# A transformer block in split fp32 on one core: weights loaded whole and split in place, in more places

## The chip, the cores and the metric

The kernel runs on one core of a Trainium2 chip. The metric is device time in microseconds (us) of one execution, as the median of several runs; lower is better. The core's engines take their instructions in program order, each its own: PE (TensorE: matmuls; "PEld" is its loading of the stationary operand), DVE (VectorE), ACT (ScalarE), POOL (GpSimd) and SP (SyncE, which here only issues transfers, DMAs). ACT and POOL issue DMAs too. Engines wait for each other through semaphores.

## The reference

```python
h = _layernorm(x) * (1 + ca) + sa
x = x + ga * (softmax_attention(h @ wqkv, 32 heads, scale 16 ** -0.5) @ wo)
h = _layernorm(x) * (1 + cb) + sb
x = x + gb * ((_silu(h @ w_gate) * (h @ w_up)) @ w_down)
```

`x` is 2048 × 512, there are 32 heads of 16, and the hidden width F of the feed-forward network (FFN) is 1792. The six rows `sa, ca, ga, sb, cb, gb` come from `silu(c) @ w_mod`. Everything is fp32.

## The kernel before

**Split products.** PE multiplies operands of a shorter float, called fp32r in the profile. To keep fp32's precision each operand is split into a high part (`hi`, the value rounded by a copy) and a low part (`lo`, the value minus `hi`). A product is then three matmuls: high by high, high by low, low by high. The helper `accumulate` lists them as the terms `(0,0), (0,1), (1,0)`, for the left and the right operand.

**Stages.** After layer norm and the q, k, v projections, attention works on 32 units: four chunks of 512 queries, times eight groups of four heads. A unit takes 16 key tiles. For each there are scores (L506, L479), a running maximum (DVE, L481), exponentials (ACT, L508) and the product with v (L521). A unit's end normalizes: a row of sums is inverted, stored, and loaded back spread over partitions (`rb`, DMA at L542). POOL then multiplies, `on` (L548), and stores (`o_dr`, L549). For the last unit ACT and DVE do that.

**FFN.** When a chunk's eight units are done, it gets the output projection with wo, a residual, a second layer norm, and the FFN. The FFN has 14 `gate_up` jobs, one for each 128 columns of F, and 7 pairs of `down` jobs, each pair with 256 rows of w_down; they go in the order gate_up 0, 1, 2, down 0, gate_up 3, 4, down 1, and so on to gate_up 13, down 6. A gate_up ends with a tanh on ACT (L773), products on DVE (L777, L779: `m`) and a split of `m` into `mid` (L781 high, L782 low): POOL does it for chunks 0 to 2, ACT and DVE for the last chunk and one more place. Down results are added to the residual at L793.

**Order.** The code's order is each engine's order; nothing else schedules. `plain(...)` emits attention alone, `filled(places, work)` emits four attention pairs and puts matmuls of the previous chunk's FFN between them. So the FFN of chunks 0 to 2 runs inside the attention of later units, and the last chunk's runs alone at the end, through `whole`, which calls `hook()` (the postponed splits of `m`) after each job. `at(i, f)` makes a function due at step i; `n` is the number of steps.

**Weights before.** During the attention of chunk 0 a generator, `split_weights`, runs on POOL: it loads the plain weights, multiplies wo and w_down by their rows `ga` and `gb`, splits all, and stores both halves to DRAM (`gu_dr`, `wd_dr`, `wo_dr`). Every chunk then loads both halves, 1 MB for each gate_up (both matrices), for each down pair and for each of two wo tiles. The loads stand on SP's queue: L652 for gate and up, one job ahead in two places (`bufs=2`); L657 for down, in one place, issued when the previous pair is done. In the last chunk gate and up have four places. The last chunk's input (`v_flat<-in_A_x`, L641) is loaded by POOL's queue, and used when the output projection is added.

Of the kernel before, what the change touches and what calls it, by code (L numbers as in the profile page):

```python
# [19 lines left out]
P = 128  # L20
S = 2048
D = 512
# [79 lines left out]
def block_kernel(ctx, tc, x, wqkv, wo, w_gate, w_up, w_down, c, w_mod, out):  # L102
# [32 lines left out]
    o_dr = dram.tile([NC, NG, P, CW], F32, name="o_dr")  # L135
    gu_dr = dram.tile([NF, P, 4, NK, P], F32, name="gu_dr")
    wd_dr = dram.tile([NF // FG, P, 2, FG, D], F32, name="wd_dr")
    wo_dr = dram.tile([NK // 2, P, 2, 2, D], F32, name="wo_dr")

# [434 lines left out]

    def split_weights():

        def raw(src, k):
            t = tile_mid().bitcast(F32)
            nc.gpsimd.dma_start(t.rearrange("p e c -> p (e c)").rearrange("p (k c) -> p k c", k=k), src)
            return t  # L580

        def parts(hi, lo, t):
            nc.gpsimd.tensor_copy(hi, t)
            nc.gpsimd.tensor_sub(lo, t, hi.bitcast(F32))

        def store(dst, w):
            nc.gpsimd.dma_start(dst, w.bitcast(F32))

        def cols(m):
            return slice(m * FG * P, (m + 1) * FG * P)  # L590

        srcs = [(wod[:, 2 * k:2 * k + 2, :], 2) for k in range(NK // 2)]
        for m in range(NF // FG):
            srcs += [(wgd[:, :, cols(m)], NK), (wud[:, :, cols(m)], NK), (wdd[:, m * FG:(m + 1) * FG, :], FG)]
        ahead = [raw(*srcs.pop(0)) for _ in range(2)]
        yield

        def following():
            if srcs:
                ahead.append(raw(*srcs.pop(0)))  # L600
            return ahead.pop(0)

        for k in range(NK // 2):
            t = following()
            nc.gpsimd.tensor_mul(t, t, ga_bc[:, None, :].to_broadcast([P, 2, D]))
            w = tile_gu()
            parts(as_wo(w)[:, 0], as_wo(w)[:, 1], t)
            store(wo_dr[k], as_wo(w))
            yield
        for m in range(NF // FG):  # L610
            ws = [tile_gu() for _ in range(FG)]
            for e in range(2):
                t = following()
                src = t.rearrange("p e c -> p (e c)").rearrange("p (k f c) -> p f k c", k=NK, f=FG)
                for f in range(FG):
                    parts(ws[f][:, 2 * e], ws[f][:, 2 * e + 1], src[:, f])
                    if e:
                        store(gu_dr[m * FG + f], ws[f])
                yield
            t = following()  # L620
            nc.gpsimd.tensor_mul(t, t, gb_bc[:, None, :].to_broadcast([P, FG, D]))
            w = tile_wd()
            parts(w[:, 0], w[:, 1], t)
            store(wd_dr[m], w)
            yield

    class Chunk:
        def __init__(self, ci, x2, oT, hT):
            self.ci, self.x2, self.oT, self.hT = ci, x2, oT, hT
            self.w, self.wd, self.mid, self.mv, self.nt = {}, {}, {}, None, []  # L630
            self.places, self.ahead, self.loaded = None, 1, set()
            self.jobs = [(gate_up, (0,)), (gate_up, (1,))]
            for m in range(NF // FG):
                if m:
                    self.jobs.append((gate_up, (2 * m + 1,)))
                if m + 1 < NF // FG:
                    self.jobs.append((gate_up, (2 * m + 2,)))
                self.jobs += [(down, (m, 0)), (down, (m, 2))]
# [4 lines left out]
        def load_wo(self, places=None):  # L643
            self.wo = places or [as_wo(tile_gu()) for _ in range(NK // 2)]
            for k, w in enumerate(self.wo):
                (nc.gpsimd if self.ci == last else nc.sync).dma_start(w.bitcast(F32), wo_dr[k])

        def load_gu(self, f):
            if f < NF and f not in self.loaded:
                self.loaded.add(f)  # L650
                self.w[f] = self.places[f % len(self.places)] if self.places else tile_gu()
                nc.sync.dma_start(self.w[f].bitcast(F32), gu_dr[f])  # L652

        def load_wd(self, m):
            if m < NF // FG:
                self.wd[m] = tile_wd()
                nc.sync.dma_start(self.wd[m].bitcast(F32), wd_dr[m])  # L657

# [130 lines left out]
    def down(ch, m, t0, outs, halves):  # L789
# [54 lines left out]
    def close_unit(u, i):  # L844
# [12 lines left out]
        if u % NG == NG - 1:  # L857
            if u // NG:
                at(i + 4, lambda: begin(u // NG))
                at(i + 5, lambda: chunks[u // NG].load_wo())  # L860
            at(i + 7, lambda: chunks[u // NG].load_o(nc.gpsimd))
            at(i + 9, lambda: chunks[u // NG].split_o())

    at(3, lambda: begin(0))
    at(UG - 2, lambda: chunks[0].load_wo())

    weights2 = split_weights()

    def after(i):
# [6 lines left out]
        if i == -2:  # L876
# [7 lines left out]
            load_q(2)  # L884
        if 0 <= i < UG and i % 16 in (3, 5, 8):
            next(weights2, None)
# [84 lines left out]
    at(n - 24, begin_last)  # L971
    at(n - 13, lambda: chunks[last].load_o(nc.gpsimd, range(NK - 1)))
    at(n - 11, lambda: chunks[last].split_o(range(NK - 1)))
    outs = [banks[b] for b in FBANKS]
    for ci in range(last):
# [11 lines left out]
        for _ in range(len(ch.jobs) - (KEEP if ci == last - 1 else 0)):  # L987
# [55 lines left out]
    run(whole(ch, ch.jobs))  # L1043
# [23 lines left out]
```

## Time and profile before

| what | us |
|---|---|
| median of 3 runs (1879.09 to 1879.83) | 1879.76 |
| profiled execution: span from its first to its last instruction | 1875.6 |
| median of the runs less that span (the profile gives no other time of the profiled execution) | 4.2 |
| PE busy in the span | 1846.7 |
| DVE busy | 1541.8 |
| ACT busy | 1252.4 |
| POOL busy | 415.3 |

The page gives for each engine its busy time, its share of the span and its number of instructions. A row of a group reads: line, engine, operation, output<-inputs, shapes, number, then busy us and mean ns of one, then the idle time just before them and what ended it. A row of the timeline reads: start, duration, engine, line, operation, number; in brackets the idle time before and what ended it. A row of the waits reads: engine, instruction, what it waited for, us in all, times, the longest. A transfer's row has the size and the us from issue to landing. In the program's time, attention without FFN work runs from about 210 to 540 us, the FFN of chunks 0 to 2 is mixed in until about 1750, and the last chunk's FFN takes 1752 to 1871.

### The profile page before, as it was taken

How to read it: one execution, taken by the hardware profiler on the slowest of the kernel's cores; microseconds unless marked ns; L12 is line 12 of the kernel's file. 1: busy time of each engine (PE TensorE's matmuls, PEld its weight loads, DVE VectorE, ACT ScalarE, POOL GpSimd, SP SyncE). 2: the span in 40 equal slices, each digit the busy share in tenths (PEclk: the TensorE clock that was granted, in tenths of full speed). 3: DMA queues.
4: the chain of work that ended last, by engine and by line, in shares of the span. 5: the costliest groups of instructions: out<-in, count | busy, mean ns of one | idle time of the engine just before them, and what ended most of it. 6: DMA issues, size and time to landing. Idle time of an engine off the chain costs nothing.

```text
span 1875.6 us, 41002 instructions
## 1 busy us (share of the span) xinstructions
PE 1846.7 (98%) x16996; PEld 1160.4 (62%) x16996; DVE 1541.8 (82%) x2558; ACT 1252.4 (67%) x2406; POOL 415.3 (22%) x498
## 2 busy tenths in 40 slices
PE   7999999999999999999999999999999999999999
PEld 5766444444455766666555667666554566667887
DVE  5548999999999888888999888889999988831643
ACT  4221888888887766777777776677878877674211
POOL 3000454456323211111133111111123011030200
PEclk9999999999999999999999999999999999999999
DMA  8855677766843534554454454453643446243642
GB/s 286 292 198 142 174 183 178 201 167 190 211 86 78 145 102 124 144 124 90 107 124 116 108 127 131 121 122 78 159 86 56 108 92 156 86 159 119 249 180 110
DMA packets 78854, 267.62 MB, mean 143 GB/s; under 512 B 17364, under 2 KB 22484, under 8 KB 57988
## 3 DMA queue, kind: packets, MB, share of 16 engines
q1 hardware_dynamic: 59820, 180.10, 33.0%
q0 software_dynamic: 18160, 84.10, 19.0%
q8 instruction: 133, 2.18, 0.5%
q10 hardware_dynamic: 688, 0.80, 0.1%
q14 instruction: 53, 0.43, 0.1%
HBM read 201.85 MB, written 62.13 MB: 141 GB/s over the span
## 4 chain that ended last, share of the span: by engine, by line
PE 95%; DVE 2%; ACT 2%; DMA 0%; issue 0%; SPq 0%; ACTq 0%; DVEq 0%
PE bank L521 26%; PE bank L506 22%; PE bank L719 19%; PE bank L479 10%; PE bank L729 7%; PE bank L209 7%; DVE mx L481 1%; PE bank L762 1%; PE bank L491 1%; PE bank L162 0%; PE bank L703 0%; DMA wm_ab<-in_w_mod 0%; DVE stt L745 0%; PE bank L279 0%; PE bank L493 0%; PE bank L492 0%
## 5 line engine op out<-in xcount | busy, mean ns | idle before, releaser
L481 DVE TENSOR_REDUCE mx<-bank 128x1 f32<-128x512 f32 x2048 | 1286.5, 682 | 119.5 <-PE bank L479 72.4
L479 PE MATMUL bank<-kop,qop 48*128 48x512 f32 x2048 | 748.0, 432 | 3.6 <-DVE mx L481 3.4
L506 PE MATMUL bank<-qop,kop 50*128 50x512 f32 x2048 | 742.1, 427 | 4.6 <-ACT pt__20499 L508 0.5
L506 PEld LDWEIGHTS bank<-qop,kop 50*128 50x128 f32 x2048 | 347.0, 184 | 305.6 <-issue 63.3
L479 PEld LDWEIGHTS bank<-kop,qop 48*128 48x128 f32 x2048 | 343.9, 184 | 30.7 <-DVE mx L481 14.4
L719 PE MATMUL bank<-act,wgu 64*128 64x512 f32 x1872 | 297.9, 392 | 0.0
L719 PEld LDWEIGHTS bank<-act,wgu 64*128 64x128 f32 x1872 | 188.4, 187 | 30.9 <-DVE m L779 0.3
L548 POOL TENSOR_TENSOR on<-o,rb 128x512 f32<-128x512 f32 x31 | 39.7, 1282 | 442.9 <-DMA rb<-d_dr 304.0
L719 PE MATMUL bank<-wd,mid 64*128 64x512 f32 x912 | 136.5, 397 | 0.0
L781 POOL CAST mid<-m 128x512 fp32r<-128x512 f32 x40 | 24.3, 609 | 430.1 <-PE bank L479 165.5
L719 PEld LDWEIGHTS bank<-wd,mid 64*128 64x128 f32 x912 | 93.3, 185 | 12.0 <-issue 0.8
L209 PE MATMUL bank<-hT,wqs 128*128 128x512 f32 x384 | 95.7, 399 | 2.1 <-DVE prt L369 0.8
L209 PEld LDWEIGHTS bank<-hT,wqs 128*128 128x128 f32 x384 | 70.3, 188 | 24.3 <-issue 6.1
L777 DVE SCALAR_TENSOR_TENSOR q<-th,bank 128x512 f32<-128x512 f32 x56 | 37.7, 673 | 57.4 <-ACT th L773 57.2
L773 ACT ACTIVATE th<-bank 128x512 f32<-128x512 f32 x56 | 33.2, 593 | 58.3 <-PE bank L729 57.9
L793 DVE TENSOR_TENSOR x<-bank,x 128x512 f32<-128x512 f32 x84 | 53.8, 684 | 20.4 <-PE bank L506 20.2
L369 DVE TENSOR_TENSOR prt<-bank,prt 128x512 fp32r<-128x512 f32 x32 | 22.0, 688 | 46.5 <-ACT prt L367 46.5
L367 ACT CAST prt<-bank 128x512 fp32r<-128x512 f32 x32 | 18.8, 587 | 60.2 <-PE bank L209 46.9
L779 DVE TENSOR_TENSOR m<-bank,q 128x512 f32<-128x512 f32 x56 | 38.7, 691 | 21.2 <-PE bank L729 19.1
L729 PE MATMUL bank<-wd,mid 128*128 128x512 f32 x216 | 52.1, 394 | 0.4 <-DVE mid L782 0.3
L782 POOL TENSOR_TENSOR mid<-m,mid 128x512 fp32r<-128x512 f32 x40 | 51.6, 1291 | 3.3
L719 PE MATMUL bank<-wgu,act 64*128 64x512 f32 x288 | 47.7, 394 | 0.1
(6282 smaller groups left out, 5155.0 us busy)
## 6 DMA issues: line engine op xcount, KB each, us to landing
wgu<-gu_dr SPq DMA_DIRECT2D x48, 1024.0 KB
wd<-wd_dr SPq DMA_DIRECT2D x28, 1024.0 KB
kop<-kd SPq DMA_DIRECT2D x33, 768.0 KB
kop<-kd POOLq DMA_DIRECT2D x29, 768.0 KB, 8.5
gu_dr<-wgu POOLq DMA_DIRECT2D x14, 1024.0 KB, 14.1
kd<-prt SPq DMA_DIRECT2D x16, 512.0 KB
qd<-prt SPq DMA_DIRECT2D x16, 512.0 KB
kop<-gu_dr SPq DMA_DIRECT2D x8, 1024.0 KB
```

Source lines behind the costliest of these rows:

```text
L209: nc.tensor.matmul(pt, lhs(a, k), rhs(b, k), start=(n == 0), stop=(n == 3 * nk - 1))
L479: nc.tensor.matmul(pm, qop[u][rows, s, qt * P:(qt + 1) * P], kop[u % 3][rows, s, kc * CW:(kc + 1) * CW], start=True, stop=True)
L481: nc.vector.tensor_reduce(mx[u][:, b, s, qt, kc:kc + 1], pm, op=ALU.max, axis=AX.X)
L506: nc.tensor.matmul(sp, kop[u % 3][rows, h // 2, kt * P:(kt + 1) * P], qop[u][rows, h // 2, :], start=True, stop=True)
L521: nc.tensor.matmul(pv[u][32 * h:32 * h + 32, cols], v_flat[:, e0:e0 + 32], p_[h][:, cols], start=(kt == 0 and half == 0), stop=(kt == 15), ...
L548: mul.tensor_mul(on, o, rb)
L719: nc.tensor.matmul(outs[e], lhs(e, a, k)[rows], rhs(b, k)[rows], start=(ph == 0 and j == 0), stop=(j == z and (ph == 1 or trade is not None)),
L729: nc.tensor.matmul(outs[e], lhs(e, a, k), rhs(b, k), start=(j == 0), stop=(j == z))
L777: nc.vector.scalar_tensor_tensor(q, th, 1.0, outs[0], op0=ALU.add, op1=ALU.mult)
L779: nc.vector.tensor_mul(m32, outs[1], q)
L782: (nc.gpsimd if slow else nc.vector).tensor_sub(mid[:, 1, :], m32, mid[:, 0, :].bitcast(F32))
L793: nc.vector.tensor_add(ch.x2[:, t, :], outs[e], ch.x2[:, t, :])
```

## The change

`split_weights` becomes `relay_weights`: wo and w_down are loaded, multiplied by their rows and stored plain; gate and up are copied plain from DRAM to DRAM, in blocks of one job. A chunk now loads the plain tile, half as many bytes (512 KB), into the low half's place, and splits it there: a copy writes the high half, a subtraction turns the place into the low half. For chunks 0 to 2, and for wo in every chunk, POOL does both. For the last chunk's gate, up and down, ACT copies and DVE subtracts (`alone`). Gate and up have three places instead of two (the last chunk seven instead of six), down has two instead of one; loads run two jobs ahead (last chunk five), and a down tile's load is issued when the pair before it starts. [...] PE's instructions and their order are the same.

```diff
@@ places
-        return pf.tile([P, 4, NK, P], F32R, name="wgu", tag="wgu", bufs=2)
+        return pf.tile([P, 4, NK, P], F32R, name="wgu", tag="wgu", bufs=3)
-        return pf.tile([P, 2, FG, D], F32R, name="wd", tag="wd", bufs=1)
+        return pf.tile([P, 2, FG, D], F32R, name="wd", tag="wd", bufs=2)
@@ the generator during chunk 0's attention
+    def relay_weights():
...
+        def scaled_out(dst, t, row):
+            nc.gpsimd.tensor_mul(t, t, row[:, None, :].to_broadcast([P, 2, D]))
+            nc.gpsimd.dma_start(dst, t)
...
+            for f in range(2 * j - 2, 2 * j):
+                if 0 <= f < NF:
+                    for e, w in enumerate((wgd, wud)):
+                        nc.gpsimd.dma_start(gu_dr[f, :, e], w[:, :, f * P:(f + 1) * P])
@@ Chunk
-            self.places, self.ahead, self.loaded = None, 1, set()
+            self.places, self.ahead, self.loaded = None, 2, set()
...
-                nc.sync.dma_start(self.w[f].bitcast(F32), gu_dr[f])
+                nc.sync.dma_start(self.w[f][:, 1::2].bitcast(F32), gu_dr[f])
+
+        def halves(self, hi, lo, alone):
+            (nc.scalar.copy if alone else nc.gpsimd.tensor_copy)(hi, lo.bitcast(F32))
+            (nc.vector if alone else nc.gpsimd).tensor_sub(lo, lo.bitcast(F32), hi.bitcast(F32))
+
+        def split_gu(self, f, alone=False):
...
+                self.halves(self.w[f][:, 0::2], self.w[f][:, 1::2], alone)
+
+        def split_wd(self, m, alone=False):
...
+                self.halves(self.wd[m][:, 0], self.wd[m][:, 1], alone)
...
-                nc.sync.dma_start(self.wd[m].bitcast(F32), wd_dr[m])
+                nc.sync.dma_start(self.wd[m][:, 1].bitcast(F32), wd_dr[m])
@@ down
-            if t0:
-                ch.load_wd(m + 1)
-
+        if t0 == 0:
+            ch.load_wd(m + 1)
@@ scaled, at the end
         ch.load_gu(0)
+        ch.load_gu(1)
...
+        ch.split_gu(0)
@@ FFN of chunks 0 to 2
-            for places in (TWO, TWO) if job is gate_up else (DOWN,):
-                filled(places, work)
-    chunks[last - 1].load_gu(NF - 2)
+            if job is not gate_up:
+                filled(DOWN, work)
+                continue
+            filled(TWO, work)
+            ch.split_gu(args[0] + 1)
+            filled(TWO, work)
+            if args[0] % FG:
+                ch.split_wd(args[0] // FG)
+    ch.load_gu(NF - 1)
+    ch.load_wd(NF // FG - 1)
+    ch.split_wd(NF // FG - 2)
     filled((0,) * 4, iter(()))
+    for f in (NF - 2, NF - 1):
+        ch.split_gu(f)
+    ch.split_wd(NF // FG - 1)
@@ whole, after hook()
+            if job is gate_up:
+                f = args[0]
+                ch.split_gu(f + 3, True)
+                if f % FG:
+                    ch.split_wd(f // FG, True)
@@ the last chunk
-    ch.places = [tile_gu() for _ in range(2)]
+    ch.places = [tile_gu() for _ in range(3)]
-    ch.ahead = 4
+    ch.ahead = 5
...
             ch.turned(banks[6 + e], k + e, nc.vector if k else nc.gpsimd)
         take(rest, 6)
+        for f in range(k, k + 2):
+            ch.split_gu(f, True)
@@ main
-    nc = _bacc.Bacc("TRN2", target_bir_lowering=False, num_devices=1)
+    nc = _bacc.Bacc("TRN2", target_bir_lowering=False, num_devices=1, dynamic_dma_scratch_size=4096)
```

Lines of `after` that do the same as lines of `before` have other numbers: L781 and L782 become L774 and L775, L777 and L779 become L770 and L772, L793 becomes L786, L719 and L729 (the FFN's matmuls) L712 and L722, L641 becomes L616. The two lines of `halves` are L630 (the copy) and L631 (the subtraction).

The change shows in the engines' order at three places. The first is POOL at gate_up 0 and 1 of chunk 0. Before, the multiply and store of a unit's output, then the splits of `m` of gate_up 0, 1:

```order
L548 TENSOR_TENSOR on<-o,rb 128x512
L549 DMA o_dr<-on 128x512
L781 CAST mid<-m_6905 128x512
L782 TENSOR_TENSOR mid<-m_6905,mid 128x512
L781 CAST mid<-m_7088 128x512
L782 TENSOR_TENSOR mid<-m_7088,mid 128x512
```

After, at the same place:

```order
L548 TENSOR_TENSOR on<-o,rb 128x512
L549 DMA o_dr<-on 128x512
L630 CAST wgu<-wgu 128x2x512
L631 TENSOR_TENSOR wgu<-wgu 128x2x512
L774 CAST mid<-m_6804 128x512
L775 TENSOR_TENSOR mid<-m_6804,mid 128x512
L630 CAST wgu<-wgu 128x2x512
L631 TENSOR_TENSOR wgu<-wgu 128x2x512
L774 CAST mid<-m_6989 128x512
L775 TENSOR_TENSOR mid<-m_6989,mid 128x512
L630 CAST wd<-wd 128x1024
L631 TENSOR_TENSOR wd<-wd 128x1024
```

The splits of gate and up tiles 1 and 2 and of down tile 0 have come in; the one of tile 1 is the next thing behind `on` and its store.

The second place is POOL ahead of the last chunk's input load. Before:

```order
L782 TENSOR_TENSOR mid<-m_20315,mid 128x512
L548 TENSOR_TENSOR on<-o,rb 128x512
L549 DMA o_dr<-on 128x512
L781 CAST mid<-m_20459 128x512
L782 TENSOR_TENSOR mid<-m_20459,mid 128x512
L641 DMA v_flat<-in_A_x 128x4x512
```

After:

```order
L631 TENSOR_TENSOR wgu<-wgu 128x2x512
L774 CAST mid<-m_20484 128x512
L775 TENSOR_TENSOR mid<-m_20484,mid 128x512
L630 CAST wd<-wd 128x1024
L631 TENSOR_TENSOR wd<-wd 128x1024
L630 CAST wgu<-wgu 128x2x512
L631 TENSOR_TENSOR wgu<-wgu 128x2x512
L630 CAST wgu<-wgu 128x2x512
L631 TENSOR_TENSOR wgu<-wgu 128x2x512
L630 CAST wd<-wd 128x1024
L631 TENSOR_TENSOR wd<-wd 128x1024
L616 DMA v_flat<-in_A_x 128x4x512
```

The first row after is the split of gate and up tile 11, which follows the same store. Between that store and the load now lie the splits of gate and up tiles 11, 12 and 13 and of down tiles 5 and 6 of chunk 2.

The third place is the end of the program on DVE, from gate_up 13's products to the first two of the last four additions. Before:

```order
L777 SCALAR_TENSOR_TENSOR q<-th,bank_69 128x512
L779 TENSOR_TENSOR m_21597<-bank_70,q 128x512
L782 TENSOR_TENSOR mid<-m_21597,mid 128x512
L793 TENSOR_TENSOR v_flat<-bank_67,v_flat 128x512
L793 TENSOR_TENSOR v_flat<-bank_68,v_flat 128x512
```

After:

```order
L770 SCALAR_TENSOR_TENSOR q<-th,bank_69 128x512
L772 TENSOR_TENSOR m_21669<-bank_70,q 128x512
L775 TENSOR_TENSOR mid<-m_21669,mid 128x512
L631 TENSOR_TENSOR wd<-wd 128x1024
L786 TENSOR_TENSOR v_flat<-bank_67,v_flat 128x512
L786 TENSOR_TENSOR v_flat<-bank_68,v_flat 128x512
```

The subtraction for down tile 6 has come in between the split of `m` and the last additions; its copy stands on ACT likewise, as the last instruction there.

More of the change, by code (lines that the diff above doesn't have):

```diff
@@ L135, in block_kernel @@
     o_dr = dram.tile([NC, NG, P, CW], F32, name="o_dr")
[L136 to L138 removed]
+    gu_dr = dram.tile([NF, P, 2, NK, P], F32, name="gu_dr")
+    wd_dr = dram.tile([NF // FG, P, FG, D], F32, name="wd_dr")
+    wo_dr = dram.tile([NK // 2, P, 2, D], F32, name="wo_dr")
     def stats(pool, xt, keep):
@@ L573, in as_wo, with raw @@
         return w.rearrange("p (b k) x c -> p b k (x c)", b=2)
-    def split_weights():
-        def raw(src, k):
+    def relay_weights():
+        def raw(src):
             t = tile_mid().bitcast(F32)
-            nc.gpsimd.dma_start(t.rearrange("p e c -> p (e c)").rearrange("p (k c) -> p k c", k=k), src)
+            nc.gpsimd.dma_start(t, src)
             return t
[L582 to L624, printed above, removed]
@@ new lines, in scaled_out @@
+        def scaled_out(dst, t, row):
+            nc.gpsimd.tensor_mul(t, t, row[:, None, :].to_broadcast([P, 2, D]))
+            nc.gpsimd.dma_start(dst, t)
+        srcs = [(wo_dr[k], wod[:, 2 * k:2 * k + 2, :], ga_bc) for k in range(NK // 2)]
+        srcs += [(wd_dr[m], wdd[:, m * FG:(m + 1) * FG, :], gb_bc) for m in range(NF // FG)]
+        ahead = []
+        for j in range(len(srcs) + 1):
+            if j < len(srcs):
+                ahead.append(raw(srcs[j][1]))
+            if j:
+                dst, _, row = srcs[j - 1]
+                scaled_out(dst, ahead.pop(0), row)
+            for f in range(2 * j - 2, 2 * j):
+                if 0 <= f < NF:
+                    for e, w in enumerate((wgd, wud)):
+                        nc.gpsimd.dma_start(gu_dr[f, :, e], w[:, :, f * P:(f + 1) * P])
@@ L972, in block_kernel @@
     at(n - 13, lambda: chunks[last].load_o(nc.gpsimd, range(NK - 1)))
+    at(n - 14, lambda: chunks[last].split_wo())
     at(n - 11, lambda: chunks[last].split_o(range(NK - 1)))
```

17 lines of the change are left out of this document (13 added, 4 removed).

## The prediction

> **What bounds the kernel now.** I read the engine shares and the chain of waits on the page first, then TensorE's (PE's) waits, then busy time by stretch, and last the timeline at the places where the change puts new work.
>
> ```profile
> span 1875.6 us, 41002 instructions
> PE 1846.7 (98%) x16996; PEld 1160.4 (62%) x16996; DVE 1541.8 (82%) x2558; ACT 1252.4 (67%) x2406; POOL 415.3 (22%) x498
> PE 95%; DVE 2%; ACT 2%; DMA 0%; issue 0%; SPq 0%; ACTq 0%; DVEq 0%
> PE bank L279 <- DMA wm_ab<-in_w_mod: 11.3, 1, 11.3
> 210.00:520.00 310.00, 309.88 (x3100) 145.35 (x3092) 307.93 (x526) 270.64 (x534) 156.04 (x156) 1.00 0.71 185
> 600.00:880.00 280.00, 280.00 (x2928) 192.01 (x2925) 243.82 (x385) 199.65 (x380) 47.46 (x54) 1.00 0.49 123
> 1752.00:1850.00 98.00, 98.00 (x430) 80.42 (x429) 41.59 (x61) 14.80 (x25) 4.65 (x7) 1.00 0.52 203
> ```
>
> The first three lines are the page's: PE is busy 98% of the span and is 95% of the chain. The fourth is PE's only long wait on a transfer; it is at the start, for the modulation weights, which the change does not touch. No wait of PE names a weight load. The last three are stretches (length; busy time and instructions of PE, PE's loader, DVE, ACT, POOL; then granted clock, DMA share, GB/s): attention with the weights prepared beside it, a chunk's FFN between attention, and the last chunk's FFN alone. PE fills all three at clock 1.00. So the 1 MB weight loads are hidden already, and halving them is worth nothing in itself. The span is 4.2 us below the median of the runs (1879.76); I make the sum against the span and add 4.2.
>
> **Taken off POOL at the start: nothing gained.** The old split goes (among it the copies and subtractions of gate/up and w_down); scaling of seven wd tiles and two wo tiles stays. In 210 to 520 POOL falls from 156 us to a few tens. DVE, not POOL, is the second full engine there:
>
> ```profile
> L481 DVE TENSOR_REDUCE mx<-bank 128x1 f32<-128x512 f32 x510 | 307.5, 677 | 1.8 <-PE bank L479 1.3 <-PE bank L506 0.3
> L481 DVE TENSOR_REDUCE mx<-bank 128x1 f32<-128x512 f32 x91 | 55.3, 678 | 0.4 <-PE bank L479 0.2
> 1440.00:1495.00 55.00, 54.94 (x560) 25.87 (x552) 54.52 (x94) 47.73 (x96) 4.92 (x6) 1.00 0.35 74
> ```
>
> The first row is that stretch, the other two are 1440 to 1495, where POOL works 4.9 of 55 us. A reduction takes 677 ns beside a busy POOL and 678 beside an idle one. Gain: 0, at most 1 ns × 510 = 0.5 us. The relay's copies from DRAM to DRAM (28 of 256 KB in 512-byte rows) run where DMA is at 0.71 and PE waits for none of it: 0.
>
> **Split of the last down tile, wd6: the one sure loss.** In the tail both new instructions of wd6 stand behind gate_up 13's, and the last down pair follows at once.
>
> ```profile
> 1864.98 1.33 PEld L729 LDWEIGHTS bank<-wd,mid 128*128 128x128 f32 x6
> 1866.13 0.62 ACT L781 CAST mid<-m 128x512 fp32r<-128x512 f32 x1 [2.81 <-DVE m L779]
> 1866.79 0.69 DVE L782 TENSOR_TENSOR mid<-m,mid 128x512 fp32r<-128x512 f32 x1 [0.69 <-ACT mid L781]
> 1866.81 0.30 PEld L729 LDWEIGHTS bank<-wd,mid 128*128 128x128 f32 x2 [0.49 <-ACT mid L781]
> 1867.53 3.52 PEld L729 LDWEIGHTS bank<-wd,mid 128*128 128x128 f32 x16 [0.43 <-DVE mid L782]
> L495 ACT CAST mr<-bank 16x256 fp32r<-16x256 f32 x32 | 11.6, 363 | 4.0 <-PE bank L493 3.9
> L536 DVE RECIPROCAL dn<-dn 128x16 f32<-128x16 f32 x32 | 7.7, 241 | 6.9 <-DMA dn<-o 6.9
> ```
>
> Now PE runs 6 of the 24 matmuls ahead, 2 after ACT's cast, and the last 16 from 1867.53, at 0.22 each. After the change ACT's cast of wd6 (128x1024) starts when the mid cast ends, 1866.75. No row has a 128x1024 cast on ACT. From 256 columns at 363 ns and 512 at 620 the slope is 1.0 ns a column: 0.62 + 512 × 1.0 = 1.13; bound above 2 × 0.62 = 1.24. It ends 1867.88, and only then has the pair any half of its weights: the first matmul (high × high) may go, the second needs the low half. DVE starts 0.04 later (as 1866.75 to 1866.79 in the rows). Its 128x1024 subtraction is bounded above by 2 × 0.69 = 1.38 and below by the slope from 16 columns (241) to 512 (690): 0.69 + 0.46 = 1.15; between, 1.26. It ends 1869.18; PE resumes 0.05 later, 1869.23, with 23 matmuls to go where it had 16 at 1867.53. Loss: 1.70 + 7 × 0.22 = 3.24, say 3.3 with the longer step when the weights change; ends 3.1 and 3.6. What follows (two additions, four stores) shifts as a whole.
>
> **Splits of the tail's other tiles: hidden.** wd5 is used one gate_up later:
>
> ```profile
> 1849.66 0.62 ACT L781 CAST mid<-m 128x512 fp32r<-128x512 f32 x1 [2.81 <-DVE m L779]
> 1854.00 5.45 PEld L729 LDWEIGHTS bank<-wd,mid 128*128 128x128 f32 x24
> ```
>
> From the end of gate_up 11's mid cast (1850.28) to the pair are 3.72 us. For wd5 alone 0.04 + 1.13 + 1.26 fit easily. For wd0 to wd4 a gate/up split (also 1024 columns) stands ahead: two casts end 2.26 after the mid cast, the second subtraction at 2.26 + 0.04 + 1.26 = 3.56, against a need at 3.72 for the high half and 3.95 for the low: 0. With both upper prices it is 0.1 late five times. Gate/up tiles have two jobs or more. This cover goes if ACT or DVE is 0.4 us later there.
>
> **Splits on POOL in the FFN stretches: hidden, thinly at two places.** A split costs POOL 1.04 + 2.38 = 3.42 us:
>
> ```profile
> L583 POOL CAST wd<-mid 128x1024 fp32r<-128x1024 f32 x7 | 7.3, 1038 | 0.5
> L584 POOL TENSOR_TENSOR wd<-mid,wd 128x1024 fp32r<-128x1024 f32 x7 | 16.7, 2380 | 0.6
> 609.64 0.42 SPq L652 DMA_DIRECT2D wgu<-gu_dr  x1
> 610.23 0.32 SPq L657 DMA_DIRECT2D wd<-wd_dr  x1
> 610.74 0.56 SPq L542 DMA_DIRECT2D rb<-d_dr  x1
> 619.87 1.29 POOL L548 TENSOR_TENSOR on<-o,rb 128x512 f32<-128x512 f32 x1 [8.43 <-DMA rb<-d_dr]
> 621.46 0.61 POOL L549 DMA_DIRECT2D o_dr<-on  x1 [0.30 <-POOL on L548]
> 623.17 0.93 PE L719 MATMUL bank<-act,wgu 64*128 64x512 f32 x6
> 1033.01 1.29 POOL L548 TENSOR_TENSOR on<-o,rb 128x512 f32<-128x512 f32 x1 [8.53 <-DMA rb<-d_dr]
> 1036.28 0.89 PE L719 MATMUL bank<-act,wgu 64*128 64x512 f32 x6
> ```
>
> 21 splits are 72 us a chunk; with the 47 of the row above POOL is at about 119 of 280, no bound. Its order matters: it takes one instruction after another, and multiplying a unit's output (on) waits for the denominators' transfer (rb), with everything queued behind. In chunk 0 the split of tile 1 stands behind that pair, which ends 622.07. Then 3.42 and gaps of 0.08: 625.57, while gate_up 1 begins 623.17 and touches the low half some five matmuls on, about 623.45: 2.1 late. But rb was itself late because two 1 MB loads were issued just ahead of it. They, with rb's 0.25 MB, took 609.64 to 619.87, 10.2 us; a 1 MB load alone takes 5.9 (below). That is 4.3 us for 1.25 MB, 3.4 a MB; one MB less lets rb land about 3.4 sooner, and two thirds of that suffice. I take 0; bounds 0 and 2.1. Chunk 1 has the same distance (1033.01 to 1036.28): again 0 to 2.1. In chunk 2 a stretch of attention alone lies between that pair and gate_up 0, so the split has time.
>
> **The last chunk's input load.** This 1 MB load stands behind five splits (gate/up tiles 11, 12, 13, wd5 and wd6 of chunk 2) on POOL's queue.
>
> ```profile
> 1699.66 0.81 POOL L641 DMA_DIRECT2D v_flat<-in_A_x  x1
> v_flat<-in_A_x POOLq DMA_DIRECT2D x1, 1024.0 KB, 5.9
> 1724.14 0.69 DVE L548 TENSOR_TENSOR on<-o,rb 128x512 f32<-128x512 f32 x1 [6.63 <-DMA rb<-d_dr]
> 1731.36 0.62 ACT L667 CAST kop<-kop 128x512 fp32r<-128x512 f32 x1 [16.07 <-DMA kop<-o_dr]
> 1732.02 0.69 DVE L668 TENSOR_TENSOR kop<-kop 128x512 fp32r<-128x512 f32 x1 [7.18 <-ACT kop L667]
> 1733.79 2.88 PE L762 MATMUL bank<-kop,kop 128*128 128x512 f32 x12
> ```
>
> Five splits are 17 us: it goes out near 1716 and lands near 1722. The block itself is wanted only after 1733.79. But it now moves beside the last unit's rb, the first link of that unit's chain (multiply 1724.14, cast 1731.36, subtraction until 1732.71, PE 1733.79). Slack is 1.1 us. When rb is issued (five us before its multiply) about half of the 1 MB is still to come, 3 us of the 5.9; shared, rb is 0 to 3 late. I take 1.4, about the middle, and thus +0.3; ends 0 and 2. The gate/up load that competes later on this chain is halved, which works the other way.
>
> **Sum.** 1875.6 + 3.3 + 0.3 = 1879.2; plus 4.2 is 1883.4 us, 3.6 us (0.19%) above 1879.76.
>
> [...] At the handover to the last chunk, VectorE's subtractions run beside POOL's:
>
> ```profile
> 1749.69 1.28 POOL L707 TENSOR_TENSOR kop<-h,kop 128x512 fp32r<-128x512 f32 x1
> 1750.14 1.38 DVE L782 TENSOR_TENSOR mid<-m,mid 128x512 fp32r<-128x512 f32 x1 [1.12 <-ACT mid L781]
> 1755.34 3.82 PE L729 MATMUL bank<-kop,wgu 128*128 128x512 f32 x16
> ```
>
> The same subtraction takes 0.69 in the tail and 1.38 beside POOL's, which had 0.83 us to go when it began. The change puts the splits of gate/up tiles 0 and 1 on DVE exactly there, ahead of the subtractions for the input's third and fourth blocks. Gate_up 0 goes through the four blocks with three matmuls each, so it wants those two after 6 and 9 matmuls of 0.23, some 1.4 and 2.1 us after 1755.34. The two DVE splits (2.5 us from 1751.52) end 1754.1, the two subtractions (0.7 each) about 1755.5, some 1.3 to 2 early. One block of 1.3 by POOL eats it, two make PE 1.3 late. I count 0. [...]
>
> **Rivals.** (B) POOL's queue or the late load decides: rb does not come earlier, or the load collides: up to 2 × 2.1 or 2 more, 1884 to 1888, around 1885.5. For it: waits of 8.43 and 8.53 on rb already; against: less is now queued ahead. (C) The blocking just weighed: 1884.7. (D) The tail costs less, because a cast or subtraction is cheaper than the slopes, or half a microsecond comes back in the first stretch: 1880 to 1882.7. (E) Faster: the DVE-paced stretch 210 to 520 speeds up once POOL is quiet. It must first pay 3.6 and then win 3.8 more: 7.4/510 = 15 ns a reduction. With 20 ns it gives 10.2, so 1873. Against it stand 677 and 678.
>
> **Chances.** 0.2% is 3.8 us, about what a measurement of this kernel tells from no change: the bounds are 1876.0 and 1883.5, and my forecast lies just below the upper. The forecast (1882.8 to 1884.1) 0.48, of it 0.31 same and 0.17 slower; B 0.27 and C 0.05, slower; D 0.13, 0.12 of it same and 0.01 faster; E 0.07. Faster 0.08, same 0.43, slower 0.49. The range 1881.5 to 1887.0 holds the forecast and C, most of B and half of D, and leaves out about 0.2.
>
> **What would show it.** In the profile after: in the tail, PE waits for DVE's wd subtraction before the last pair, with 23 matmuls behind it, and DVE's row is 1.15 to 1.38; ACT's cast of 1024 columns 1.13; the other tail pairs without a wait; rb landing some 3 us sooner near 619, and no wait of PE for POOL's wgu; the reductions still 677; the load of the last input near 1716 and the last unit's cast within 1.4 of its place. I am wrong if PE shows waits for POOL's splits in chunks 0 to 2, or if reductions in the first stretch fall by over 10 ns.

## The result, and the profile after

| | median us | runs | ratio to before | 95% interval |
|---|---|---|---|---|
| before | 1879.8 | 6 | | |
| after | 1885.6 (1883.82 to 1887.24) | 6 | 1.0033 | 1.0021 to 1.0044 |

The changed kernel is slower by 0.33%. It lies inside the predicted range, 2.2 us above the predicted 1883.4, on the far side of the bound for "same". The profiled execution took 1885.19 us with a span of 1883.4, so 1.8 us lie around the span. One run of e5 below took 5478 us and is left out of its median.

The page of the changed kernel, span, engine shares and chain of waits:

```profile
span 1883.4 us, 41134 instructions
PE 1852.2 (98%) x16996; PEld 1164.8 (62%) x16996; DVE 1565.8 (83%) x2579; ACT 1271.6 (68%) x2427; POOL 575.8 (31%) x566
PE 94%; ACT 2%; DVE 2%; DMA 2%; SPq 0%; issue 0%; ACTq 0%; DVEq 0%
```

PE's four longest waits, and below them the one for DVE's subtraction (us in all, times, the longest):

```profile
PE bank L279 <- DMA wm_ab<-in_w_mod: 10.5, 1, 10.5
PE bank L722 <- ACT wd L630: 2.4, 1, 2.4
PE bank L479 <- DVE mx L481: 1.9, 6, 0.3
PE bank L755 <- ACT kop L660: 1.0, 1, 1.0
...
PE bank L722 <- DVE wd L631: 0.8, 1, 0.8
```

Three waits are new: two for the split of wd6 (ACT's copy, then DVE's subtraction), one for the cast of the last unit's output. (A wait of 0.8 us for a load of keys, `kop`, near 132 us, was not in the first profile of the kernel before but is in two others of it, e5 and e6 below, with 1.2 and 1.3.) No wait of PE names a split on POOL. The stretches:

```profile
600.00:880.00 280.00, 280.00 (x2923) 193.27 (x2923) 243.08 (x383) 198.86 (x379) 112.01 (x92) 1.00 0.40 84
1752.00:1850.00 98.00, 97.98 (x430) 79.64 (x429) 63.96 (x81) 33.60 (x46) 9.02 (x10) 1.00 0.34 112
```

The reductions of the first attention stretch, 210 to 520 us, among the groups of lines:

```profile
L481 DVE TENSOR_REDUCE mx<-bank 128x1 f32<-128x512 f32 x509 | 306.9, 678 | 2.1 <-PE bank L479 1.0 <-PE bank L506 0.8
```

PE still fills both stretches; POOL went from 47 to 112 us in the first of them (119 was forecast). In the attention stretch, where POOL went from 156 to 75 us, a reduction takes 678 ns where it took 677.

The tail, in the timeline after:

```profile
1869.23 0.62 ACT L774 CAST mid<-m 128x512 fp32r<-128x512 f32 x1 [2.82 <-DVE m L772]
1869.75 1.04 ACT L630 CAST wd<-wd 128x1024 fp32r<-128x1024 f32 x1
...
1870.83 1.22 DVE L631 TENSOR_TENSOR wd<-wd 128x1024 fp32r<-128x1024 f32 x1 [0.26 <-ACT wd L630]
1870.85 0.19 PEld L722 LDWEIGHTS bank<-wd,mid 128*128 128x128 f32 x1 [2.82 <-ACT wd L630]
...
1872.11 6.74 PEld L722 LDWEIGHTS bank<-wd,mid 128*128 128x128 f32 x23 [1.07 <-DVE wd L631]
```

It is the forecast picture: one matmul after the copy, 23 after the subtraction. But the loads of the 23 take 6.74 us, 0.29 each, where those of the 16 before took 0.22. The stretches of the tail (length, busy times, then the granted clock) tell why:

```profile
1868.00:1872.00 4.00, 0.96 (x4) 0.22 (x2) 2.56 (x3) 1.56 (x2) 0.00 (x0) 1.00 0.00 0
1872.00:1876.00 4.00, 3.89 (x11) 3.09 (x12) 0.74 (x2) 0.00 (x0) 0.00 (x0) 0.63 0.00 0
1876.00:1880.00 4.00, 3.29 (x13) 2.30 (x12) 2.06 (x3) 0.00 (x0) 0.00 (x0) 0.94 0.34 131
```

Right after PE's idle time its granted clock averages 0.63 over 4 us, and 0.94 over the next 4. Finer stretches show it at 0.50 from 1873.1 on and at 1.00 again from 1876.5: it was low for 3.4 us. In that time the starts of successive matmuls lie 0.43 apart, before and after it 0.23.

If one compares the start of the same matmul in both profiles, the lag of the changed kernel jumps by 1.6 us at the last unit's output (1735.8) and by 3.8 at the last down pair, and grows by 1.1 over its remaining matmuls. The rest is a start 1.3 us earlier, a slow growth of 2 us over 1500 us, and another 0.7 between 1736 and the last pair. The slow growth is looked at with e3 and e5 below.

### The profile page after: what moved, and what is told of

It is laid out like the page before. It is cut to its first block, busy times and chain, and to the rows that moved or that the text cites. A ratio compares the mean times of both kernels' runs of the same rounds, so it can differ in the third digit from the quotient of the medians.

```text
span 1883.4 us, 41134 instructions
## 1 busy us (share of the span) xinstructions
PE 1852.2 (98%) x16996; PEld 1164.8 (62%) x16996; DVE 1565.8 (83%) x2579; ACT 1271.6 (68%) x2427; POOL 575.8 (31%) x566
## 4 chain that ended last, share of the span: by engine, by line
PE 94%; ACT 2%; DVE 2%; DMA 2%; SPq 0%; issue 0%; ACTq 0%; DVEq 0%
PE bank L521 26%; PE bank L506 23%; PE bank L712 19%; PE bank L479 9%; PE bank L722 7%; PE bank L209 6%; DVE mx L481 1%; PE bank L491 1%; PE bank L696 0%; PE bank L162 0%; PE bank L279 0%; DVE stt L738 0%; PE bank L493 0%; PE bank L492 0%; DMA wm_ab<-in_w_mod 0%; DMA rb<-d_dr 0%
## 5 line engine op out<-in xcount | busy, mean ns | idle before, releaser
L712 PE MATMUL bank<-act,wgu 64*128 64x512 f32 x1872 | 301.9, 393 | 0.0
L712 PEld LDWEIGHTS bank<-act,wgu 64*128 64x128 f32 x1872 | 191.3, 187 | 28.9 <-DVE m L772 0.3
L712 PE MATMUL bank<-wd,mid 64*128 64x512 f32 x912 | 136.8, 397 | 0.0
L631 POOL TENSOR_TENSOR wgu<-wgu 128x1024 fp32r<-128x1024 f32 x48 | 114.5, 2385 | 4.0
L774 POOL CAST mid<-m 128x512 fp32r<-128x512 f32 x40 | 24.4, 610 | 261.4 <-PE bank L479 160.8
L712 PEld LDWEIGHTS bank<-wd,mid 64*128 64x128 f32 x912 | 93.2, 186 | 12.4 <-issue 1.2
L770 DVE SCALAR_TENSOR_TENSOR q<-th,bank 128x512 f32<-128x512 f32 x56 | 37.6, 672 | 46.7 <-ACT th L766 46.5
L786 DVE TENSOR_TENSOR x<-bank,x 128x512 f32<-128x512 f32 x84 | 53.9, 685 | 20.8 <-PE bank L712 10.5
L404 POOL DMA_DIRECT2D kop<-kd x29 | 17.0, 586 | 147.0 <-PE bank L479 81.2
L722 PE MATMUL bank<-wd,mid 128*128 128x512 f32 x216 | 54.3, 406 | 3.2 <-ACT wd L630 2.4
L775 POOL TENSOR_TENSOR mid<-m,mid 128x512 fp32r<-128x512 f32 x40 | 51.7, 1291 | 3.2
```

Source lines behind the costliest of these rows:

```text
L631: (nc.vector if alone else nc.gpsimd).tensor_sub(lo, lo.bitcast(F32), hi.bitcast(F32))
L712: nc.tensor.matmul(outs[e], lhs(e, a, k)[rows], rhs(b, k)[rows], start=(ph == 0 and j == 0), stop=(j == z and (ph == 1 or trade is not None)),
L722: nc.tensor.matmul(outs[e], lhs(e, a, k), rhs(b, k), start=(j == 0), stop=(j == z))
L770: nc.vector.scalar_tensor_tensor(q, th, 1.0, outs[0], op0=ALU.add, op1=ALU.mult)
L775: (nc.gpsimd if slow else nc.vector).tensor_sub(mid[:, 1, :], m32, mid[:, 0, :].bitcast(F32))
L786: nc.vector.tensor_add(ch.x2[:, t, :], outs[e], ch.x2[:, t, :])
```

## The experiments

Theory A: the loss sits in two places, the split of wd6 at the end and the late input load. Theory K: PE's idle time there also lowers its clock. Rival R: the splits cost a little everywhere.

| version | median us | ratio to before | 95% interval |
|---|---|---|---|
| e1: wd6 split early | 1882.27 | 1.0014 | 1.0005 to 1.0023 |
| e2: input load on SP's queue | 1885.91 | 1.0033 | 1.0021 to 1.0046 |
| e3: both | 1880.87 | 1.0006 | 0.9997 to 1.0015 |
| e4: spare matmuls before the last pair | 1884.78 | 1.0025 | 1.0014 to 1.0036 |
| e5: before, unchanged | 1881.08 | 1.0011 | 1.0002 to 1.0020 |
| e6: before, late input load | 1882.47 | 1.0016 | 1.0007 to 1.0024 |
| e7: e3, copies on POOL twice | 1883.24 | 1.0021 | 1.0012 to 1.0029 |
| e8: e3, loads of 1 MB | 1891.48 | 1.0069 | 1.0057 to 1.0081 |
| e9: e4 and e2 together | 1884.19 | 1.0026 | 1.0016 to 1.0036 |
| e10: e4 again | 1883.64 | 1.0023 | 1.0012 to 1.0033 |
| e11: after again | 1886.90 | 1.0034 | 1.0022 to 1.0047 |

Each ratio is to runs of the kernel before in the same series: their medians are 1880.06 (e1 to e4), 1880.05 (e5 to e8) and 1878.81 (e9 to e11, on another chip). Across series the ratios compare better than the medians. The row e5 is a warning: the same kernel against itself gives 1.0011, with an interval that leaves out 1. Differences of 0.1%, 2 us, are at the edge of what these times tell. Smaller ones are read from the profiles.

**Split wd6 early.**

```diff
-                if f % FG:
+                if f % FG and f < NF - 1:
                     ch.split_wd(f // FG, True)
+            elif args == (NF // FG - 2, 2):
+                ch.split_wd(NF // FG - 1, True)
```

> The changed kernel with one edit: down tile 6 of the last chunk is split after the down pair before gate_up 13, not behind gate_up 13. Theory A (two places: the split of wd6 at the end, and the last chunk's input load beside the last unit's output chain): TensorE's waits of 2.4 and 0.8 us before the last pair go, 3.8 us at the matmuls' starts; with theory K (the clock granted to TensorE fell to 0.63 because it stood idle there, and nine matmuls took 0.43 us instead of 0.23) another 1.2 to 1.6 us: 1880 to 1881 against 1885.6. A without K: 1881.8. Rival theory R (the splits cost time everywhere, by contention, so that moving one tile gives little): not below 1884.5.

It gave 1882.27, 3.3 below the changed kernel's first median; by the ratios it is 0.19 to 0.20% (3.6 to 3.8 us) below both series of the changed kernel. Of PE's loads in the tail:

```profile
1871.03 1.36 PEld L722 LDWEIGHTS bank<-wd,mid 128*128 128x128 f32 x6
1872.86 0.30 PEld L722 LDWEIGHTS bank<-wd,mid 128*128 128x128 f32 x2 [0.46 <-ACT mid L774]
1873.58 3.55 PEld L722 LDWEIGHTS bank<-wd,mid 128*128 128x128 f32 x16 [0.43 <-DVE mid L775]
```

This is the pattern 6, 2, 16 of the kernel before, with 0.22 each: both waits for wd6 are gone and the clock stays at 1.00. R as the cause of the whole loss, which allowed no less than 1884.5, falls. The median is 1.3 above the upper end of A with K, and 0.5 above A without K, so something is left; see e3.

**Input load on SP's queue**, which no split blocks.

```diff
-    ch.load_x2(nc.gpsimd)
+    ch.load_x2(nc.sync)
```

> The changed kernel with one edit: the last chunk's input load goes by SP's queue, where no split stands ahead of it, and not by POOL's. Theory A: it goes out near 1700, the last unit's denominators are loaded near 1719 again and not at 1723, TensorE's wait of 1.0 us for the last unit's cast goes, and the time falls by 1.2 to 1.5 us, to about 1884.2. Rival R: the chain is late for another reason (the transfers of the splits' own loads), it stays near 1735 and the time does not change.

The load does not go out near 1700: on SP it stands behind the load of wd6, which waits for its place until 1711.25, and leaves at 1711.62. That is early enough: PE's wait for the last unit's cast is gone, and the lag in the profile shrinks by 1.55 us there. The time did not fall. In this profile the low clock after the tail's wait lasted longer than in the first one (0.50 from 1872 to 1876, still 0.74 over the four us that follow; 6.8 us in all, not 3.4), which costs some 1.1 us more (the last 23 matmuls' loads took 7.84 us, not 6.74) and eats most of the gain.

**Both.**

> The changed kernel with the two edits together. Theory A with K: 1885.6 less 4.8 to 5.4 less 1.2 to 1.5, 1879 to 1879.6, the same as the kernel before within 0.1%. If R holds beside it (a slow drift of about 2 us over the whole run, seen between the two profiles): 1880.5 to 1882.

Its edits are the two above, no other. 1880.87, ratio 1.0006 with 1 inside the interval: the two edits give back most of the loss. But the forecast of A with K, at most 1879.6, is missed, and the median lies in the range given for R beside it. The interval leaves room for 2.8 us. The rest of the change (63 gate, up and down splits on POOL beside attention, 14 gate and up and six down splits on ACT and DVE, half the load traffic, `dynamic_dma_scratch_size=4096`) does not move these medians by an amount that they tell from none.

The profiles tell more. The FFN's gate and up matmuls in the kernel before, in its second profile (e5), in the changed kernel and in e3:

```profile
L719 PE MATMUL bank<-act,wgu 64*128 64x512 f32 x1872 | 297.9, 392 | 0.0
L719 PE MATMUL bank<-act,wgu 64*128 64x512 f32 x1872 | 297.7, 392 | 0.0
L712 PE MATMUL bank<-act,wgu 64*128 64x512 f32 x1872 | 301.9, 393 | 0.0
L712 PE MATMUL bank<-act,wgu 64*128 64x512 f32 x1872 | 300.7, 393 | 0.0
```

Three profiles of before (with e6) have 297.6 to 297.9, the changed kernel and the variants e1 to e4 and e9 to e11 have 300.1 to 301.9. These are busy times that overlap with attention's, so not all of the difference is time lost. The time lost is in the starts: against the first profile of before, the lag grows between 600 and 1700 us by 0.2 and 0.3 in e5 and e6, and by 0.9 to 2.9 in those eight. So R holds in a small form: by these profiles the change costs some 1 to 2 us beside its two places, spread over PE's matmuls and mostly without a wait (the medians leave 0.8, and cannot tell). Why is not shown; no run takes the POOL splits, the halved loads and `dynamic_dma_scratch_size` apart there.

**PE kept busy.** Twelve matmuls that nobody reads ahead of the last pair, four behind its first:

```diff
...
+            if ch.ci == last and args == (NF // FG - 1, 0):
+                spare(12)
+                next(steps)
+                spare(4)
```

> The changed kernel with 12 spare matmuls in front of the last down pair and 4 behind its first matmul, on a bank that nobody reads, so that TensorE does not stand idle while it waits for wd6's split. Theory K: the last 22 matmuls take 0.23 us each and the end comes 1.2 to 1.6 us earlier, about 1884.2, although there is more work. If the lower clock there has another cause than the idle time: the nine slow matmuls stay, 1885.6 to 1886.

The tail's loads in the second profile of this version (e10):

```profile
1871.68 5.19 PEld L722 LDWEIGHTS bank<-wd,mid 128*128 128x128 f32 x23 [0.17 <-DVE wd L631]
```

The stretch with the waits there, with the granted clock:

```profile
1870.00:1874.00 4.00, 4.00 (x19) 3.16 (x18) 1.51 (x3) 0.37 (x1) 0.00 (x0) 1.00 0.00 0
```

The two waits are filled, the clock stays at 1.00, and the 23 matmuls' loads take 5.19 us, 1.55 less than the 6.74 of the changed kernel. The first profile (e4) and e9's have 5.19 too. K holds: with the waits filled the clock did not fall. What the runs show of it: in the changed kernel the clock was at 0.50 for 3.4 us, and there matmuls started 0.43 us apart instead of 0.23, behind two waits of 2.4 and 0.8 us with one matmul between; in e2 and e11, behind waits of 2.4 and 0.7, it was at 0.50 for 6.8 us. What sets the length is not shown. In time e4 gained less than this: 1884.78 is 0.8 below the changed kernel's first median, at the edge of what the medians tell.

**The kernel before once more**, with no edit.

> The kernel before once more, unchanged, for a second profile of it. All profiles of the changed kernel and its variants fall back against the one profile of before by about 2 us, evenly from 266 to 1700 us. Theory A: that is the one execution (its span of 1875.6 stood 4.2 us under the median, while for the others span and time are 1.8 apart); a second profile of before falls back by 1 to 3 us as well, and the time is 1880 as before. Rival R (the splits cost time everywhere): the second profile lies on the first within 0.5 us.

It fell back by 3.3 us against the first profile of itself: 0.7 by 516 us, 1.0 by 688, and 2.0 between 1757 and 1861, there 0.0044 us on each of 456 matmuls. It also began 1.4 us ahead and lost that from 133 to 137 us, where its clock was at 0.50 behind a wait of 1.2 us; the first profile has a wait of 1.6 us there and no low clock. So executions of one kernel differ by this much, and the first profiled one of before was a quick one (its span of 1875.6 belongs to about 1877.4 by the 1.8 us of the others). A expected an even loss, and the loss was in these places: e5 does not have the slow growth between 600 and 1700 us (0.2), so it does not explain that of the changed kernel.

**The kernel before with a late input load.**

```diff
+    idle = pf.tile([P, CW], F32, name="idle", tag="idle", bufs=1)
+    nc.gpsimd.memset(idle, 0.0)
+    for _ in range(13):
+        nc.gpsimd.tensor_sub(idle, idle, idle)
     ch.load_x2(nc.gpsimd)
```

> The kernel before with one thing added: 13 idle subtractions of 1.29 us each on POOL ahead of the last chunk's input load, so that it goes out near 1717 as in the changed kernel. Theory A: the small transfers of the last unit's chain wait beside this 1 MB load, TensorE waits 1.0 to 1.5 us for the last unit's cast: 1881 to 1881.5 against 1880. If the late load is harmless: 1880, and the cast stays near 1731.4.

The load went out at 1715.27, and PE has the new wait without any other part of the change:

```profile
PE bank L762 <- ACT kop L667: 1.8, 1, 1.8
```

The time rose to 1882.47, by 2.4 against the runs of before beside it and 1.4 against e5, more than the 1881 to 1881.5 expected. What the load collides with is shown by the DMA issues on ACT's queue. Ahead of the transfer of the denominators (rb) stand the load of the row of sums (L532) and the store of their inverse (L537, a few KB). First before, then after:

```profile
1717.55 0.35 ACTq L537 DMA_DIRECT2D d_dr<-dn  x1
1719.03 0.56 ACTq L542 DMA_DIRECT2D rb<-d_dr  x1
```

```profile
1717.43 0.81 POOL L616 DMA_DIRECT2D v_flat<-in_A_x  x1
1718.09 0.35 ACTq L537 DMA_DIRECT2D d_dr<-dn  x1
1723.04 0.56 ACTq L542 DMA_DIRECT2D rb<-d_dr  x1
1735.14 0.62 ACT L660 CAST kop<-kop 128x512 fp32r<-128x512 f32 x1 [19.30 <-DMA kop<-o_dr]
```

Between the small store and the load that needs it lie 1.5 us before and 5.0 after, with 1 MB issued 0.7 us ahead of the store. In e6 the load of the sums was hit: 5.5 us to the store, where 2.2 was usual. In e11 the issue of the 1 MB began at 1719.88, 0.4 us ahead of the store's, and the store was not late (1.5 us to the next issue); only rb was hit (7.1 us to the next issue, not 5.8), and PE had no wait at this place at all. So the price here is 0 to 1.8 us: PE's wait was 0 with the 1 MB issued 0.4 us ahead of the store (e11), 1.0 with 0.7 (the changed kernel), and 1.8 with 0.6 ahead of the load of the sums (e6).

**Copies on POOL twice** (for chunks 0 to 2, on the version e3).

```diff
             (nc.scalar.copy if alone else nc.gpsimd.tensor_copy)(hi, lo.bitcast(F32))
+            if not alone and self.ci < last:
+                nc.gpsimd.tensor_copy(hi, lo.bitcast(F32))
```

> The version with both edits (wd6 split early, input load on SP's queue; 1880.9), and every copy of a split on POOL for chunks 0 to 2 made twice, so that a split takes 4.46 us and not 3.42. The prediction gave the splits as hidden, with no slack left at two places (gate_up 1 of chunks 0 and 1) and 2 us or more at nearly all others: 1 us at each of the two, 1882.5 to 1883.5. If POOL's order has slack everywhere: 1881. If it has none anywhere (a split each 13 us on the path): 10 us and more, above 1890.

1883.24, 2.4 above e3. Its lag against e3 jumps at the two places, by 1.0 at 623 and by 1.1 at 1037 us. (It also grows by 2.1 near 580 and by 0.5 near 995 us, where PE's clock was low in e7's profile, whose mean is 0.997 where e3's is 0.999; near 578 e6 and e11, which have no second copy, show that too.) PE's wait for POOL's subtraction in e7, in all and at the first place:

```profile
PE bank L714 <- POOL wgu L633: 1.5, 3, 0.7
```

```profile
625.60 0.50 PE L714 MATMUL bank<-act,wgu 64*128 64x512 f32 x2 [0.64 <-POOL wgu L633]
```

The other splits of the FFN stretches took 1.04 us more each, and PE waited for one of them, 0.2 us at 1263. That the two places have little slack shows without the second copy too: in e1 and e11 PE waited 0.1 us for POOL's subtraction at the first.

**Full loads** (for chunks 0 to 2, on e3): the plain tile is loaded into both places, and the copy overwrites one.

```diff
+                if self.ci < last:
+                    nc.sync.dma_start(self.w[f][:, 0::2].bitcast(F32), gu_dr[f])
                 nc.sync.dma_start(self.w[f][:, 1::2].bitcast(F32), gu_dr[f])
```

and the same for the down tiles.

> The version with both edits, and for chunks 0 to 2 each gate, up and down load made twice (the plain tile also into the high half's place, which the copy then overwrites), so that 1 MB per tile is moved as before. The prediction held that the split of tile 1 behind the multiplication by the denominators is hidden only because halved loads let these land sooner. Theory A: the denominators near 617 land 2 to 3 us later again, and TensorE waits at gate_up 1 of chunks 0 and 1, 1.5 to 2.2 us each: 1884 to 1885.5. If the denominators come early for another reason: 1881.

1891.48, 10.6 above e3: the mechanism as forecast, at three times its size. From the issue of rb to POOL's multiplication pass 9.1 us before (610.74 to 619.87), 6.7 in the changed kernel, and 9.1 again here. The changed kernel on POOL, and then e8 on POOL and PE:

```profile
616.83 1.29 POOL L548 TENSOR_TENSOR on<-o,rb 128x512 f32<-128x512 f32 x1 [6.27 <-DMA rb<-d_dr]
...
620.16 2.39 POOL L631 TENSOR_TENSOR wgu<-wgu 128x1024 fp32r<-128x1024 f32 x1
```

```profile
621.69 1.29 POOL L548 TENSOR_TENSOR on<-o,rb 128x512 f32<-128x512 f32 x1 [9.78 <-DMA rb<-d_dr]
...
624.99 0.73 PE L716 MATMUL bank<-act,wgu 64*128 64x512 f32 x4 [1.09 <-POOL wgu L632]
627.42 0.79 PE L716 MATMUL bank<-act,wgu 64*128 64x512 f32 x2 [1.70 <-POOL wgu L633]
```

The four microseconds in e8 behind these waits:

```profile
626.00:630.00 4.00, 2.58 (x12) 2.09 (x14) 0.70 (x2) 0.64 (x2) 3.92 (x4) 0.65 0.09 36
```

PE waits for the copy and for the subtraction, and the clock falls again, to 0.65, behind waits of 1.09 and 1.70. So each place costs about 5 us (the lag grows from 0.2 to 5.1, and from 6.1 to 11.5) instead of 2, and a third place, at 685 us, costs 1. The two extra issues on SP also put rb's issue later, 612.60, so not all of this is the doubled bytes.

**The spare matmuls with the input load on SP's queue (the edits of e4 and e2), beside e4 and the changed kernel unchanged.**

> The changed kernel with the spare matmuls ahead of the last pair and the input load on SP's queue. The load's own price is still open: the profile of the version with that edit alone shows the 1.5 us won, but its time was unchanged, and there 16 of the last 23 matmuls ran at the lower clock where the changed kernel had nine. With TensorE kept busy that difference cannot arise. If the load costs what the profiles show: 1.3 to 1.6 us below the version with spare matmuls alone. If it costs nothing in time: equal to it within 0.5 us.

> The version with the spare matmuls alone once more, beside the one before and the one after: 1884.3 to 1885.3, and 0.5 to 1.5 below the changed kernel, whose low clock it avoids.

> The changed kernel once more, beside the two versions: 1885 to 1886.3, with a low clock after TensorE's wait in the tail whose length (nine matmuls in the first profile) may differ from execution to execution.

e9 gave 1884.19 and e10 1883.64: in time the input load's move shows nothing even with the clock held at 1.00, though e9's profile has no wait for the last unit's cast and e10's has one of 1.1 us. Of the pairs, e3 against e1 says 1.4 us, e6 1.4 to 2.4, e2 and e9 none. The wait is shown, and that it comes from the late load is shown; what it costs in the median lies between 0 and about 2 us and is not settled. e10 lies below its range and e11 above its own, 3.3 us apart by the medians and 0.11% (2.1 us) by the ratios; e11's five runs lie between 1882.56 and 1888.60. The last 23 matmuls' loads in e11, and the clock there:

```profile
1872.69 7.84 PEld L722 LDWEIGHTS bank<-wd,mid 128*128 128x128 f32 x23 [1.07 <-DVE wd L631]
1872.00:1876.00 4.00, 3.30 (x8) 2.63 (x9) 0.64 (x1) 0.00 (x0) 0.00 (x0) 0.50 0.00 0
1876.00:1880.00 4.00, 4.00 (x14) 3.15 (x13) 1.38 (x2) 0.00 (x0) 0.00 (x0) 0.68 0.33 129
```

They took 7.84 us, so there the low clock cost 2.65 and not 1.55: its length varies between executions, and e11 and e10 differ by more than the first such pair for that reason at least in part.

## Why the prediction was right, and where it was short

- **The number.** The forecast was 3.6 us of loss, and 5.8 were measured. The result lies above the forecast's own stretch (1882.8 to 1884.1) and at the 1885.5 of rival B. Half of B came, the late load's collision; its other half, waits for POOL's splits, did not. The rest came from the clock and from the spread loss of 1 to 2 us, which the sum has at nothing. So it was in part luck that the range held.
- **What bounds the kernel.** Right: PE fills the stretches (280.00 of 280 and 97.98 of 98 us), no weight load was waited for, and nothing became faster with half the loads.
- **POOL's relief at the start.** Right: 678 ns a reduction for 677; rival E (faster) had no ground.
- **wd6.** Right in place and order. The copy took 1.04 (1.13 forecast), the subtraction 1.22 (1.26). The two waits move the last pair by 3.8 us at its start; the kernel before lost 0.6 us inside the pair, to its own waits for mid, which now do not occur, so 3.2 stay of the 3.3 forecast. The 3.3 is 3.24 rounded up for a longer step when the weights change, and no run shows such a step: in the kernel before, the 24 weight loads of a whole pair, one for each matmul, take 5.45 us, 0.23 each.
- **The step that was missing** stands behind it: "1.70 + 7 × 0.22" prices the 23 matmuls at the speed of a PE that did not stand still. They took 0.29 each, 1.55 us more in all, and 2.65 more in another execution.
- **The tail's other splits.** Right: no wait of PE for wd0 to wd5 or for a gate or up tile there. The working's 3.56 starts the second subtraction while the first still runs; one behind the other (0.04 + 1.13 + 2 × 1.26) they end at 3.69, still ahead of 3.95.
- **Splits on POOL.** Right that PE does not wait for them, and for the reason given: rb came 2.4 us sooner after its issue (3.4 was forecast from two rows), the two places had no microsecond left (e7), and the cover is the halved loads (e8). The upper bound of 2.1 for each place was too low: in e8 the lateness was larger and the clock fell behind it. (The low half is wanted four matmuls, some 0.47 us, after the start, so about 623.64 and not 623.45.) The term 0 was too small all the same: the matmuls of these stretches started later by 1 to 2 us more in all (e3).
- **The last chunk's input load.** Issued at 1717.43 (1716 forecast). Taken as +0.3 with ends 0 and 2; the wait was 1.0, and 0 to 1.8 in other executions. The cast came 3.8 us later (1735.14 for 1731.36), 0.8 of it the lag of the whole program, where the sign of being right was 1.4. The step "rb is 0 to 3 late" named the wrong transfer: it was the small store ahead of rb, 3.5 us late.
- **Beside POOL's subtractions.** The two DVE splits at the handover took 3.55 us together, where two alone take 2.4 (1.22 each in the tail), and POOL's subtraction beside them 2.15 instead of 1.28:

```profile
1754.37 3.55 DVE L631 TENSOR_TENSOR wgu<-wgu 128x1024 fp32r<-128x1024 f32 x2 [0.24 <-ACT wgu L630]
1754.68 2.15 POOL L700 TENSOR_TENSOR kop<-h,kop 128x512 fp32r<-128x512 f32 x1
...
1759.54 2.59 PEld L722 LDWEIGHTS bank<-kop,wgu 128*128 128x128 f32 x12 [0.18 <-DVE kop L700]
```

  Side by side they took 1.15 and 0.87 us longer than alone; why is not shown, and C's blocks of 1.3 were an estimate from the 1.28 of one POOL subtraction. It used up the slack: the weight load in the last row waited 0.2 us, but the lag of the matmuls does not jump there (2.68 before, 2.71 after). So C was close to deciding and did not.
- **The sum.** 4.2 us were added for what lies around the span. It is 1.8 in every execution whose time and span are both known; the other 2.4 are most likely the luck of one profiled execution. The error did not harm the difference, since span and median were both taken of before.

## What to carry to other kernels

Here the splits taken off the loads made PE wait 0.1 us at most (e1, e11) in chunks 0 to 2, where POOL had room (112 of 280 us busy), and 3.2 us at the one place where the consumer follows at once: look there first, at the last tile of the program above all, and put its preparation one job earlier. When PE has a wait of two or three us, price the matmuls behind it too: here 23 of them cost 1.55 and 2.65 us more at the lower clock. When a queue gets new work, ask of each DMA behind it what it will meet when it goes out later, small stores in a chain first: here the reader of one started 5.0 us later instead of 1.5.

## What the runs showed that was not expected

- PE's clock: behind two waits of 2.4 and 0.8 us (2.4 and 0.7 in e2 and e11) with a matmul between, the granted clock was 0.50 for 3.4 us in the changed kernel and for 6.8 in e2 and e11, and in the tail matmuls took 0.43 us instead of 0.23. In e8, behind waits of 1.09 and 1.70 with four matmuls between, it averaged 0.65 over 4 us. In e5 it was at 0.50 from 133 to 137 us, behind a single wait of 1.2 us; the first profile of the kernel before has a wait of 1.6 us there and 1.00. The length at 0.50 differs between executions of one kernel: 1.55 and 2.65 us lost on the same 23 matmuls.
- A store of 8 KB, issued 0.7 us behind a 1 MB load on another queue, let its reader start 5.0 us later instead of 1.5. In e1, e4 and e10 (0.6, 0.7 and 1.3 us behind) it was 4.2, 5.1 and 5.0; in e11 (0.4 us behind) 1.5.
- Three profiles of the kernel before and eight of the changed kernel and its variants fall into two groups: the lag of the same matmuls grows by 0 to 0.3 us between 600 and 1700 us in the first, by 0.9 to 2.9 in the second. No experiment says why.
- Two series of runs of the same kernel (e5 against before) differ by 0.11% with an interval of 0.02 to 0.20%, about as much as the intervals claim to tell apart.
